# Attention pair on one core: the short turn of the products moved by one, and head weighing tied to VectorE's copies

## The chip, the core and the metric

The kernel runs on one core of a Trainium2 chip. TensorE (PE) multiplies into PSUM; its weight loads are listed as PEld. ScalarE (ACT) does most exponentials. VectorE (DVE) copies, and does a few exponentials by arithmetic. GpSimd (POOL) masks and weighs heads. SyncE (SP) issues the transfers. The metric is device time in microseconds (us) of one launch; the kernel before takes 1421.66 us, the median of three runs (1420.84 to 1422.12).

## The reference

Two attention layers over 2048 tokens of width 576 with 32 heads of 18, side by side in the output:

```python
def _A_ref(x, wq, wk, wv, wo):           # one key and value head for all 32 query heads
    scores = jnp.einsum("bhqd,bkd->bhqk", q, k) * (Dh ** -0.5)
    p = _softmax(scores, axis=-1)
    o = jnp.einsum("bhqk,bkd->bhqd", p, v)
    return o.transpose(0, 2, 1, 3).reshape(B, S, H * Dh) @ wo
...
def _B_ref(x, wq, wk, wv, wo, beta):     # causal within 4 segments of 512, and a memory of the segments before
    for s in range(N):
        p = _softmax(logits, axis=-1)
        a_dot = jnp.einsum("bhqk,bhkd->bhqd", p, vs)
        a_mem = num / den
        o = g * a_mem + (1.0 - g) * a_dot
        ...
    return o @ wo
...
return jnp.concatenate([a, b], axis=-1)
```

## The kernel before

The first part of the program (up to about 290 us) projects queries, keys and values, and sums the memory of B. The second part is the attention. It is cut into **blocks**: 32 A blocks (512 queries of 4 heads against all 2048 keys) and 32 B blocks (512 queries of 4 heads within their segment). B blocks come in pairs, put behind 13 of the A blocks by the list `after`.

A block is made of **items**. An item of scores is a key tile of 128 and a pair of heads: two matmuls into a score buffer E (three buffers in PSUM), then an exponential into a tile P. An A block has 32 such items, a B block 6. An item of products is a key tile and a half of the queries: four matmuls, one for each head, of P with the values, added up in O. There are as many items of products as of scores.

The work goes in **turns**, written out by the main loop (the order on TensorE, ScalarE and VectorE is the order in the code). A turn k does the scores of `turns[k]`, then their exponentials, then a piece of the output projection (`run_fill`, the filler F), then one step of VectorE's own exponential if one stands in the list `slow`, then the products of `prods[k - 2]`. `split` cuts a block's items into threes; where two are left over, as in A, that short turn is put at the place `cut`. For A, `turns` has it at place 10, the last of eleven turns, and `prods` at place 8. I number a block's turns from 0.

Of a turn's three score items, the first and the third go from E through ScalarE straight into P. The second is first copied by VectorE into a tile W, which frees E early, and ScalarE reads W last. In turn 0 of an A block the second item is VectorE's: it computes the exponential in one instruction on E (tile PD) and six later steps (`exponentials`), which the loop takes one at a turn.

When a chunk of 512 queries has all its heads, the **planner** (`at`, `due`, `finish`) loads the sums and the heads, and asks GpSimd to weigh each of five tiles of heads (`weigh`: one product for A and for the first segment of B, two products and a sum for the others). `due` takes at most two weighing steps in a turn (`heavy = 2`), and none when one of the next three turns has B blocks. GpSimd's instructions are kept in program order, but start as soon as what they wait for is there. The weighed heads are what the filler multiplies with the output weights. GpSimd also masks the exponentials of B on the diagonal (L941).

Lines of the profile: L918 and L927 scores of A and B, L936 ScalarE's exponentials, L933 the copy W, L894 to L901 VectorE's exponential, L966 products, L975 the copy of O, L773 filler, L797 its copy, L761 weighing.

Of the kernel before, what the change touches and what calls it, by code (L numbers as in the profile page):

```python
# [74 lines left out]
def attention_pair_kernel(ctx, tc, a_xT, a_w, a_wo, b_xT, b_w, b_wo, b_beta, ident_d, hmask_d, bmask_d, cmask_d, sel_d, zmask_d, selx_d, sely_d, out):  # L75
    nc = tc.nc
# [79 lines left out]
    with ExitStack() as ph:  # L156
# [248 lines left out]
        for s in range(NSEG):  # L405
# [110 lines left out]
            if not last:  # L516
                e = p2.tile([128, 4, DH], F32, name="ph31")
# [92 lines left out]
    with tc.If(loose > 0, preferred_fallthrough_block=False):  # L610
        with ExitStack() as ph:
# [37 lines left out]
            with tc.For_i(0, H, 1) as h:  # L649
# [5 lines left out]
                for i in range(NKT):  # L655
                    s, j = divmod(i, 4)
                    n = 128 * (j + 1)
# [97 lines left out]
    def weigh(ab, c, t, tiles):  # L755

        o, (rb, *mem) = parts[ab, c][: RT[t], t], [x[: RT[t]] for x in tiles]

        def step(dst, a, b, op):

            return lambda: tc.keep_in_program_order(nc.gpsimd.tensor_tensor(dst, a, b, op=op))  # L761

        steps = [step(o, o, rb, ALU.mult)]
        if mem:
            nb, rb2 = mem
            steps += [step(nb, nb, rb2, ALU.mult), step(o, o, nb, ALU.add)]
        return steps
# [117 lines left out]
        vseg[s] = v  # L885


    slow, now = [], [0]

    def exponentials(p, e):  # L890

        y, u, w = p.bitcast(U32), pp.tile([128, 2, 512], F32, name="n", bufs=1), pp.tile([128, 2, 512], F32, name="q", bufs=1)
        v, stt = nc.vector, nc.vector.scalar_tensor_tensor
        v.tensor_scalar(y, e, EXP_A, EXP_B, op0=ALU.mult, op1=ALU.add)  # L894
        steps = [
            lambda: v.tensor_scalar(u.bitcast(U32), y, MANTISSA, ONE_BITS, op0=ALU.bitwise_and, op1=ALU.bitwise_or),
            lambda: v.tensor_scalar(w.bitcast(U32), y, EXPONENT, None, op0=ALU.bitwise_and),
            lambda: stt(p, u, POLY[0], u, op0=ALU.add, op1=ALU.mult),
            lambda: stt(p, p, POLY[1], u, op0=ALU.add, op1=ALU.mult),
            lambda: stt(p, p, POLY[2], p, op0=ALU.add, op1=ALU.mult),  # L900
            lambda: stt(p, p, POLY[3], w, op0=ALU.add, op1=ALU.mult),  # L901
        ]
        slow.extend((now[0] + 2 + i, p, step) for i, step in enumerate(steps))

    def scores(it, pr, copied):

        ab, c, hg, kt = it
        st = stacks[ab, c, hg // 2]
        h = 2 * (hg % 2) + pr
        e = psE.tile([128, 2, 512], F32, name="E")  # L910
        dve = ab == "A" and (kt, pr) in BY_DVE
        p = pp.tile([128, 2, 512], F32, name="PD" if dve else "P", bufs=1 if dve else PBUFS)
        state[it, pr] = p
        n = 512 if ab == "A" else 512 - 128 * kt if kt < 2 else 384
        if ab == "A":
            for j, r0 in enumerate(HALF):
                rows = slice(r0, r0 + KR)
                nc.tensor.matmul(e[:, j], kstA[rows, 128 * kt : 128 * kt + 128], st[rows, h, :], start=True, stop=True)  # L918
            if (kt, pr) in BY_DVE:
                exponentials(p, e)  # L920
                return lambda: None
        else:
            for k, c0 in BKEYS[kt]:
                ks = slice(128 * k, 128 * k + 128)
                for j, r0 in enumerate(HALF):
                    rows = slice(r0, r0 + KR)
                    nc.tensor.matmul(  # L927
                        e[:, j, c0 : c0 + 512 - 128 * k], st[rows, 4 + h, ks], st[rows, h, 128 * k :], start=True, stop=True
                    )
        src = e  # L930
        if copied:
            src = pp.tile([128, 2, 512], F32, name="W", bufs=2)
            nc.vector.tensor_copy(src[:, :, :n], e[:, :, :n])  # L933

        def exponential():
            nc.scalar.activation(p[:, :, :n], src[:, :, :n], AF.Exp, scale=SCALE)  # L936
            if ab == "B":

                m = len(BKEYS[kt])
                diag = p.rearrange("p a (b t) -> p a b t", t=256)[:, :, 0:m, 0:128]  # L940
                nc.gpsimd.affine_select(  # L941
                    diag, diag, pattern=[[0, 2], [0, m], [1, 128]], base=0, channel_multiplier=-1, compare_op=ALU.is_ge, fill=0.0
                )

        return exponential
# [61 lines left out]
    turns, prods = [], []  # L1007
# [5 lines left out]
    def due(k, most=2, heavy=2):  # L1013

        cost = 0

        near = [its[n][0] for t in turns[k : k + 3] for n, pr in t]
        heavy *= "B" not in near
        for e in [e for e in later if e[0] <= k]:
            if most and cost + e[1] <= heavy and e[2]():  # L1020
                later.remove(e)
                e[3](k)
                cost += e[1]
                most -= 1
        return cost
# [53 lines left out]
    def split(n, cut):  # L1079

        sizes = [3] * (n // 3)
        if n % 3:
            sizes.insert(cut, n % 3)
        return [sum(sizes[:i]) for i in range(len(sizes) + 1)]

    with tc.manual_schedule(engines={ENG.PE, ENG.Activation, ENG.DVE}):
# [3 lines left out]
        for n, b in enumerate(blocks):  # L1090
            ms = [m for m in range(len(its)) if block_of[m] == n]
            items = [(m, k) for m in ms for k in range(2)]
            for out_, cut in ((turns, len(items) // 3), (prods, len(items) // 3 - 2)):
                at_ = split(len(items), cut)
                out_ += [items[a:z] for a, z in zip(at_, at_[1:])]
        at(ASK + 4, 0, lambda: True, lambda k: load_qf(2))
# [13 lines left out]
        for k in range(len(turns) + 2):  # L1110
            now[0] = k
            exps = [scores(its[n], pr, i == 1) for i, (n, pr) in enumerate(turns[k])] if k < len(turns) else []
            for i in (0, 2, 1) if len(exps) == 3 else range(len(exps)):
                exps[i]()
            if memory is None:
                run_fill()
            elif k >= ASK and all(its[n][0] == "A" for n, pr in turns[k]) and next(memory, None) is None:
                memory = None

            ends = k > 1 and any(hf and its[n][3] == (NKT - 1 if its[n][0] == "A" else 2) for n, hf in prods[k - 2])  # L1120
            if slow and (slow[0][0] <= k or not ends):
                slow.pop(0)[2]()
            for n, hf in prods[k - 2] if k > 1 else []:
                ab, c = its[n][:2]
                hg = products(its[n][:3], its[n][3], hf)
                if hg in (6, 7):
                    finish(k, ab, c, hg)
                if hg == 7 and ab == "B" and c + 1 < NSEG:
                    load_vseg(c + 1)
            due(k)  # L1130
            if k == len(turns):
                halve_w(0)
            for n, pr in turns[k] if k < len(turns) else []:
                it = its[n]
                ab = it[0]
                if pr == 0:
                    prefetch(ab, keys[ab].index((ab, it[1], it[2] // 2)) + 2)
                    if it in (("A", 0, 2, 8), ("A", 0, 5, 8)):
                        load_wo(*(("B", b_wo) if it[2] == 2 else ("A", a_wo)))

        while fill and fill[0][0] in begun:
            due(k, 4)
            run_fill()
            if filled[0] % FILL == 0:
                fill.pop(0)
            k += 1
# [25 lines left out]
        for t in range(5):  # L1172
            if t:
                halve_w(t)
            due(k, 4)
            k += 1
            halve_heads(rows[0], t)
# [5 lines left out]
        for n, key in enumerate(rows):  # L1183
            end = key == rows[-1]
            banks = [psE.tile([128, 2, 512], F32, name="E") for _ in range(3)]
            dst = [bk[:, hf, :288] for bk in banks for hf in range(2)]
# [75 lines left out]
```

## Time and profile before

| | us |
|---|---|
| median of three runs | 1421.66 |
| the profiled execution, time | 1422.47 |
| the profiled execution, span | 1420.7 |
| TensorE busy | 1404.0 |
| ScalarE busy | 1205.4 |
| VectorE busy | 964.4 |
| GpSimd busy | 244.6 |

The granted clock of TensorE was 0.997 of full speed over the span. A row of a timeline gives the start, the time that it took, engine, line, operation, tiles, shapes and count, and in brackets the engine's idle time before it with what ended it. On ScalarE and TensorE an instruction overlaps the next one, so the distance of two starts is the cost of one. A matmul of the products has two records in the trace, so an item of products (four matmuls) stands there as eight. In a row of groups or of a line's view the numbers behind a name are idle time in us and how often.

### The profile page before, as it was taken

Reading aid. Unit: us, or ns where it says so; the run is one execution under the profiler, and the core shown is the slowest. Engines: PE = TensorE matmul, PEld = TensorE weight load, DVE = VectorE, ACT = ScalarE, POOL = GpSimd, SP = SyncE. Lnnn points to the kernel's source line nnn. Section 1 sums busy time; section 2 is a strip of 40 time slices with the busy share of each in tenths; the row PEclk is TensorE's granted clock in tenths of the full one; section 3 lists DMA queues with packets and bytes.
Section 4 is the critical chain, followed back from the end, with each engine's and each line's share of the span. In section 5 each row is a group of like instructions: output and inputs, shape, how many; then the busy total and the mean of one; then the engine's idle time right before and its main releaser. Section 6 shows DMA issues by size and latency. Waiting matters only on the chain.

```text
span 1420.7 us, 39951 instructions
## 1 busy us (share of the span) xinstructions
PE 1404.0 (99%) x17132; PEld 843.3 (59%) x17132; DVE 964.4 (68%) x1157; ACT 1205.4 (85%) x1447; POOL 244.6 (17%) x326
## 2 busy tenths in 40 slices
PE   9999999999999999999999999999999999999998
PEld 6788888745555555555555555555555555555558
DVE  6656456456677767776766777666767766777663
ACT  4543434479999999999999999999999999999991
POOL 2431000003313213221110160131011400100002
PEclk9999999999999999999999999999999999999999
DMA  9766546557564535332312543232104221110013
GB/s 283 253 216 188 166 146 214 174 171 214 156 214 159 165 120 166 91 109 77 110 58 70 166 128 92 62 107 80 51 34 132 67 76 44 60 45 18 9 59 112
DMA packets 90720, 172.63 MB, mean 122 GB/s; under 512 B 14576, under 2 KB 22889, under 8 KB 90110
## 3 DMA queue, kind: packets, MB, share of 16 engines
q1 hardware_dynamic: 84122, 160.01, 36.0%
q0 software_dynamic: 1664, 4.78, 1.3%
q10 hardware_dynamic: 4752, 5.24, 1.1%
q8 instruction: 135, 2.21, 0.7%
q14 instruction: 47, 0.39, 0.1%
HBM read 99.32 MB, written 70.67 MB: 120 GB/s over the span
## 4 chain that ended last, share of the span: by engine, by line
PE 68%; ACT 7%; issue 2%; DMA 1%; DVE 1%; SPq 0%; ACTq 0%; DVEq 0%
PE O L966 31%; PE E L918 20%; PE F L773 11%; ACT P L936 7%; PE E L927 3%; PE E L1163 2%; PE F L829 1%; DMA stB<-qB 0%; DVE W L933 0%; PE F L1163 0%; PE O L1163 0%; DMA oA<-oe 0%; DMA stB<-kB 0%; DMA sm<-oA 0%; SPq L696 0%
## 5 line engine op out<-in xcount | busy, mean ns | idle before, releaser
L936 ACT ACTIVATE P<-E 128x1024 f32<-128x1024 f32 (+1 forms) x800 | 780.8, 1059 | 12.7 <-PE E L918 12.3
L933 DVE COPY W<-E 128x1024 f32<-128x1024 f32 (+1 forms) x384 | 461.2, 1201 | 248.8 <-PE E L918 189.2
L966 PE MATMUL O<-P,VA 128*32 128x256 f32 x7936 | 508.8, 380 | 0.0
L936 ACT ACTIVATE P<-W 128x1024 f32<-128x1024 f32 (+1 forms) x384 | 426.3, 1110 | 3.4 <-DVE W L933 3.2
L966 PEld LDWEIGHTS O<-P,VA 128*32 128x32 f32 x7936 | 262.2, 110 | 147.6 <-issue 6.6
L918 PE MATMUL E<-stA,kstA 56*128 56x512 f32 x1920 | 329.4, 439 | 1.8 <-DVE W L933 1.1
L918 PEld LDWEIGHTS E<-stA,kstA 56*128 56x128 f32 x1920 | 154.7, 184 | 178.2 <-ACT P L936 113.7
L941 POOL TENSOR_SCALAR_AFFINE_SELECT P<-P 128x256 f32<-128x256 f32 (+1 forms) x192 | 95.0, 495 | 480.3 <-ACT P L936 446.9
L761 POOL TENSOR_TENSOR o<-o,rb 126x512 f32<-126x512 f32 (+1 forms) x55 | 79.9, 1468 | 408.9 <-DMA o<-oA 146.0
L773 PE MATMUL F<-woB,o 126*32 126x192 f32 (+1 forms) x1920 | 127.4, 338 | 0.3 <-DVE osb L797 0.3
L966 PE MATMUL O<-P,vseg 128*32 128x256 f32 (+2 forms) x1536 | 81.8, 344 | 0.8 <-issue 0.8
L773 PEld LDWEIGHTS F<-woB,o 126*32 126x32 f32 (+1 forms) x1920 | 38.2, 108 | 70.6 <-issue 63.6
L975 DVE COPY oe<-O 128x512 f32<-128x512 f32 x64 | 44.3, 692 | 41.8 <-PE O L966 41.0
L252 PE MATMUL pj<-xh,wBl 128*126 128x512 f32 x180 | 72.4, 403 | 0.0
L252 PE MATMUL pj<-xh,wBh 128*126 128x512 f32 x180 | 71.9, 400 | 0.0
L121 ACT CAST qp<-pj 126x512 fp32r<-126x512 f32 (+1 forms) x54 | 31.0, 585 | 46.1 <-DVE kmB L450 32.4
L966 PEld LDWEIGHTS O<-P,vseg 128*32 128x32 f32 x1536 | 49.1, 109 | 25.4 <-issue 2.9
L773 PE MATMUL F<-woA,o 126*32 126x192 f32 (+1 forms) x960 | 63.9, 338 | 0.0
L927 PE MATMUL E<-stB 56*128 56x256 f32 (+3 forms) x512 | 61.3, 347 | 1.4 <-ACT P L936 0.9
L122 DVE TENSOR_TENSOR qp<-pj,qp 126x512 fp32r<-126x512 f32 (+1 forms) x54 | 36.7, 685 | 35.6 <-ACT qp L121 35.3
L252 PE MATMUL pj<-xl,wBh 128*126 128x512 f32 x144 | 57.3, 399 | 0.0
L927 PEld LDWEIGHTS E<-stB 56*128 56x128 f32 x512 | 38.6, 185 | 31.1 <-ACT P L936 20.8
(194 smaller groups left out, 1387.8 us busy)
## 6 DMA issues: line engine op xcount, KB each, us to landing
stB<-kB SPq DMA_DIRECT2D x96, 144.0 KB
stB<-qB SPq DMA_DIRECT2D x32, 288.0 KB
stA<-qA SPq DMA_DIRECT2D x30, 288.0 KB
oA<-oe SPq DMA_DIRECT2D x32, 256.0 KB
oB<-oe SPq DMA_DIRECT2D x32, 256.0 KB
qA<-qp SPq DMA_DIRECT2D x16, 504.0 KB
kB<-qp SPq DMA_DIRECT2D x16, 504.0 KB
qB<-qp SPq DMA_DIRECT2D x16, 504.0 KB
```

What stands on the lines that cost most here:

```text
L121: hold(nc.scalar.copy(qp[:R, 0, :n], src))
L122: hold(nc.vector.tensor_tensor(qp[:R, 1, :n], src, qp[:R, 0, :n].bitcast(F32), op=ALU.subtract))
L252: nc.tensor.matmul(dst, w[:, c0 : c0 + M], x, start=i == 0, stop=i == len(ops) - 1)
L761: return lambda: tc.keep_in_program_order(nc.gpsimd.tensor_tensor(dst, a, b, op=op))
L773: nc.tensor.matmul(dst[32 * j : 32 * j + 32], parts[ab, c][: RT[t], t, r0 : r0 + 32], wo[ab][: RT[t], t, c0 : c0 + n], start=start, stop=stop,
L918: nc.tensor.matmul(e[:, j], kstA[rows, 128 * kt : 128 * kt + 128], st[rows, h, :], start=True, stop=True)
L927: nc.tensor.matmul(e[:, j, c0 : c0 + 512 - 128 * k], st[rows, 4 + h, ks], st[rows, h, 128 * k :], start=True, stop=True)
L933: nc.vector.tensor_copy(src[:, :, :n], e[:, :, :n])
L936: nc.scalar.activation(p[:, :, :n], src[:, :, :n], AF.Exp, scale=SCALE)
L941: nc.gpsimd.affine_select(diag, diag, pattern=[[0, 2], [0, m], [1, 128]], base=0, channel_multiplier=-1, compare_op=ALU.is_ge, fill=0.0)
L966: nc.tensor.matmul(o[32 * j : 32 * j + 32, q0 : q0 + n], v, p[:, j % 2, p0 : p0 + n], start=m == hf == 0, stop=last and hf == 1,)
L975: nc.vector.tensor_copy(osb, o)
```

## The change

Three edits. The cut for the products' short turn moves from place 8 to place 9 of eleven; with the lag of two turns its products are multiplied in the first turn of the following block, where they were in the last turn of their own. A weighing step on GpSimd waits for the newest copy W that the loop has issued (`gate`). And `due` takes no weighing step when an entry of `slow` is due in this turn or the next.

```diff
         def step(dst, a, b, op):
 
-            return lambda: tc.keep_in_program_order(nc.gpsimd.tensor_tensor(dst, a, b, op=op))
+            def run():
+                ins = tc.keep_in_program_order(nc.gpsimd.tensor_tensor(dst, a, b, op=op))
+                if gate:
+                    tc.add_manual_dep(ins.ins, gate[-1].ins.name, AFTER, reason="beside the copies of this turn")
+
+            return run
...
-    slow, now = [], [0]
+    slow, now, gate = [], [0], []
+    AFTER = mybir.DependencyInfo(mybir.DependencyClass.Sync, mybir.DependencyReason.SCHED_ONLY)
...
-            nc.vector.tensor_copy(src[:, :, :n], e[:, :, :n])
+            gate.append(nc.vector.tensor_copy(src[:, :, :n], e[:, :, :n]))
...
-        heavy *= "B" not in near
+        heavy *= "B" not in near and all(e[0] > k + 1 for e in slow)
...
-            for out_, cut in ((turns, len(items) // 3), (prods, len(items) // 3 - 2)):
+            for out_, cut in ((turns, len(items) // 3), (prods, len(items) // 3 - 1)):
```

What that does to the order. First TensorE from an A block to the next (turn 10 of (A,3,2) and turn 0 of (A,3,3)). E with stA are scores, F the filler, O the products; PD is the tile that VectorE filled. Before:

```order
L918 MATMUL E<-stA,kstA 128x512 x4
L773 MATMUL F<-woB,o 32x192 x4
L966 MATMUL O<-P,VA 32x256 x2
L966 MATMUL O<-PD,VA 32x256 x2
L966 MATMUL O<-P,VA 32x256 x2
L966 MATMUL O<-PD,VA 32x256 x2
L918 MATMUL E<-stA,kstA 128x512 x6
L773 MATMUL F<-woB,o 32x192 x4
L966 MATMUL O<-P,VA 32x256 x12
```

and now:

```order
L924 MATMUL E<-stA,kstA 128x512 x4
L778 MATMUL F<-woB,o 32x192 x4
L972 MATMUL O<-P,VA 32x256 x2
L972 MATMUL O<-PD,VA 32x256 x2
L972 MATMUL O<-P,VA 32x256 x2
L972 MATMUL O<-PD,VA 32x256 x2
L972 MATMUL O<-P,VA 32x256 x4
L924 MATMUL E<-stA,kstA 128x512 x6
L778 MATMUL F<-woB,o 32x192 x4
L972 MATMUL O<-P,VA 32x256 x8
```

One product item, four matmuls, has moved from behind the six score matmuls of turn 0 to ahead of them. Next TensorE from an A block to a B block ((A,2,4) to (B,3,6)), where E with stB are the scores of B, before:

```order
L966 MATMUL O<-PD,VA 32x256 x2
L927 MATMUL E<-stB 128x512 x4
L927 MATMUL E<-stB 128x384 x2
L773 MATMUL F<-woB,o 32x192 x4
L966 MATMUL O<-P,VA 32x256 x12
```

and now:

```order
L972 MATMUL O<-PD,VA 32x256 x2
L972 MATMUL O<-P,VA 32x256 x4
L933 MATMUL E<-stB 128x512 x4
L933 MATMUL E<-stB 128x384 x2
L778 MATMUL F<-woB,o 32x192 x4
L972 MATMUL O<-P,VA 32x256 x8
```

The same item stands ahead of the first scores of B. Last GpSimd at the weighing of the second segment of B, with the semaphores that each instruction waits for in brackets (DMAHW are transfers, Pool is GpSimd itself). Before:

```order
L761 TENSOR_TENSOR o<-o,rb 126x512 [waits DMAHW3_49,DMAHW4_49,DMAHW1_49,DVE_49]
L761 TENSOR_TENSOR rb<-rb 126x512 [waits DMAHW5_49,DMAHW2_49]
L761 TENSOR_TENSOR o<-o,rb 126x512 [waits DMAHW6_49]
L761 TENSOR_TENSOR o<-o,rb 126x512 [waits DMAHW1_49]
L761 TENSOR_TENSOR o<-o,rb 126x512 [waits Pool_49]
```

and now:

```order
L762 TENSOR_TENSOR o<-o,rb 126x512 [waits DMAHW3_49,DMAHW4_49,DMAHW1_49,DVE_49]
L762 TENSOR_TENSOR rb<-rb 126x512 [waits DMAHW5_49,DMAHW2_49,DVE_49]
L762 TENSOR_TENSOR o<-o,rb 126x512 [waits DMAHW6_49]
L762 TENSOR_TENSOR o<-o,rb 126x512 [waits DMAHW1_49,DVE_49]
L762 TENSOR_TENSOR o<-o,rb 126x512 [waits Pool_49]
```

The instructions and their order are the same; the first of each turn now also waits for VectorE (a second one in the same turn stands behind it).

## The prediction

> **What bounds the kernel now.** I read the page first, then the busy time of a late stretch, then the timeline of TensorE, ScalarE and VectorE over one joint between two A blocks, then the same joint from A to B, then a stretch in which GpSimd weighs heads.
>
> The page's first part:
>
> ```profile
> PE 1404.0 (99%) x17132; PEld 843.3 (59%) x17132; DVE 964.4 (68%) x1157; ACT 1205.4 (85%) x1447; POOL 244.6 (17%) x326
> ```
>
> and one row of the busy-time view by stretches (its columns are PE, PEld, DVE, ACT, POOL, then granted clock and DMA):
>
> ```profile
> 1150.00:1250.00 100.00, 100.00 (x1418) 52.41 (x1410) 73.47 (x74) 99.28 (x108) 7.12 (x5) 1.00 0.18 53
> ```
>
> In the attention part TensorE and ScalarE are both filled. So neither bounds alone; they wait for each other at certain turns. The timeline of TensorE shows where. These are turns 9 and 10 of block (A,3,2), then turns 0, 1 and the start of turn 2 of (A,3,3). A turn begins with its scores (E, L918), then one piece of the output projection (F, L773), then its products (O, L966):
>
> ```profile
> 1227.34 1.08 PE L918 MATMUL E<-stA,kstA 56*128 56x512 f32 x6
> 1230.11 0.72 PE L918 MATMUL E<-stA,kstA 56*128 56x512 f32 x4
> 1230.76 0.53 PE L773 MATMUL F<-woA,o 72*32 72x192 f32 x8
> 1232.09 1.21 PE L918 MATMUL E<-stA,kstA 56*128 56x512 f32 x6
> 1233.23 0.53 PE L773 MATMUL F<-woB,o 126*32 126x192 f32 x8
> 1233.58 1.48 PE L966 MATMUL O<-P,VA 128*32 128x256 f32 x24
> 1234.99 0.96 PE L918 MATMUL E<-stA,kstA 56*128 56x512 f32 x6
> 1237.64 0.96 PE L918 MATMUL E<-stA,kstA 56*128 56x512 f32 x6
> ```
>
> Starts of E give the turns: turn 9 2.77 us, turn 10 1.98, turn 0 2.90, turn 1 2.65. Three scores cost 0.96 us when nothing holds them (turn 1), and 1.21 in turn 0: there TensorE waits about 0.25 us for a score buffer. ScalarE at the same place:
>
> ```profile
> 1230.39 1.21 ACT L936 ACTIVATE P<-W 128x1024 f32<-128x1024 f32 x1
> 1231.34 1.17 ACT L936 ACTIVATE P<-E 128x1024 f32<-128x1024 f32 x1
> 1232.24 1.21 ACT L936 ACTIVATE P<-W 128x1024 f32<-128x1024 f32 x1
> 1233.19 2.10 ACT L936 ACTIVATE P<-E 128x1024 f32<-128x1024 f32 x2
> 1235.53 1.94 ACT L936 ACTIVATE P<-E 128x1024 f32<-128x1024 f32 x2 [0.25 <-PE E L918]
> ```
>
> ScalarE's exponentials overlap: they follow each other by 0.90 us after one that reads E and by 0.95 after one that reads W (1231.34 to 1232.24, 1230.39 to 1231.34). Turns 1 to 9 hold three of them, 2.75 us. Turns 0 and 10 hold two, since VectorE does one of turn 0. Left alone, the exponential of 1235.53 would have followed at about 1233.19 + 0.90 + 0.92 = 1235.01. So ScalarE runs dry for about half a microsecond at every such joint; the page's "idle" of 0.25 is only what stands beyond the overlap. The path through a joint is: ScalarE's exponential at 1231.34 frees a score buffer, TensorE finishes the scores of turn 0, the filler, three products, the first score of turn 1, and then ScalarE starts, 0.54 us after that turn began (1234.99 to 1235.53). From there to turn 10 ScalarE is never dry and holds TensorE (2.77 instead of 2.65).
>
> **The products' short turn.** An A block has 32 score items and 32 product items, in ten turns of three and one of two. The scores' short turn is the block's last. Products lag two turns, and their list had its short turn at place 8, so it fell on turn 10, beside the short scores. Now it stands at place 9 and falls on the next block's first turn. One product item moves from turn 0 into turn 10. Nothing is added; the stores and the copy of the finished O stay in turn 1.
>
> What an item costs: turn 1 (three scores, three products, 2.65 us) less turn 10 (two and two, 1.98) is 0.67 us. The score's share is 0.96 - 0.72 = 0.24, so a product item is 0.43 us.
>
> Between two A blocks. Turn 10 becomes 1.98 + 0.43 = 2.41 us, and turn 0's scores start at 1232.52 in place of 1232.09. The buffer that held them is free when the exponential of 1231.34 is done, at 1231.34 + 1.17 = 1232.51; the second score needs it at 1232.52 + 0.24 = 1232.76, so the wait of 0.25 goes. Turn 0 then takes 2.65 - 0.43 = 2.22 us and turn 1 starts at 1234.74, not at 1234.99: **0.25 us gained**. What is late next? ScalarE's first exponential of turn 0 can start at 1232.52 + 0.54 = 1233.06, ahead of 1233.19 where ScalarE comes free, so it isn't starved there. In turn 1 ScalarE starts 0.54 after 1234.74, still some 0.27 later than it could: the joint stays TensorE's and the whole 0.25 shows. There are 18 joints from A to A (32 A blocks, 13 of them followed by B, and the last): 18 x 0.25 = 4.5 us. The two product items left in turn 0 need exponentials of turn 9, the last at 1230.39, long done.
>
> From A to B. The scores of an A block's turn 10, of the first and the second B turn behind it, and of the second B block's first turn:
>
> ```profile
> 1045.92 0.73 PE L918 MATMUL E<-stA,kstA 56*128 56x512 f32 x4
> 1047.91 1.13 PE L927 MATMUL E<-stB 56*128 56x512 f32 x6
> 1050.73 0.85 PE L927 MATMUL E<-stB 56*128 56x384 f32 x10
> 1053.27 0.90 PE L927 MATMUL E<-stB 56*128 56x512 f32 x6
> ```
>
> and ScalarE in turn 1 of the next A block:
>
> ```profile
> 1061.08 1.02 ACT L936 ACTIVATE P<-E 128x1024 f32<-128x1024 f32 x1 [0.56 <-PE E L918]
> ```
>
> The same six matmuls take 1.13 us after A and 0.90 later: 0.23 us is a wait that a product item in front of it would fill. Behind it TensorE sets the pace until ScalarE runs dry at the next A block's turn 1 (0.56 idle), so 0.23 us stays gained. The first three joints from A to B lie where the chain that ended last runs on ScalarE (two of its rows):
>
> ```profile
> 370.25 2.26 ACT P L936 x3
> 418.71 2.26 ACT P L936 x3
> ```
>
> There I count nothing. Ten are left: 10 x 0.23 = 2.3 us. From B to A nothing changes: B's six items have no short turn. Sum of this part: **-6.8 us**.
>
> **The planner's new term** (`heavy` off while an exponential step is due within a turn). Stepping through the rules: a step is due at block turn + 2 + i, but is taken as soon as a turn doesn't end a block's products; step 0 goes in turn 0, step i in turn i + 1. When `due` asks in any turn the next step's number is always at least k + 2, so the term never says no. The weighing steps stand in the same turns as before, 29 of the 65 ahead of the last rows in turns 2 to 6, which hold exponential steps. This edit costs and brings nothing, and the change doesn't do this half of what it says.
>
> **The added wait.** What the wait does change is when GpSimd starts. Before, a weighing step ran as soon as its data had landed; now it also waits for the copy W of its turn. Behind it on GpSimd stand further weighing steps and, at the next B block, the masks (L941); the planner keeps three turns free ahead of B, so the masks don't queue behind it. GpSimd in turns 3 to 5 of (A,1,6):
>
> ```profile
> 825.66 3.52 POOL L761 TENSOR_TENSOR rb<-rb 126x512 f32<-126x512 f32 x2
> 829.15 4.58 POOL L761 TENSOR_TENSOR o<-o,rb 126x512 f32<-126x512 f32 x2
> ```
>
> VectorE beside it:
>
> ```profile
> 825.89 2.16 DVE L898 SCALAR_TENSOR_TENSOR PD<-n 128x1024 f32<-128x1024 f32 x1
> 827.97 1.21 DVE L933 COPY W<-E 128x1024 f32<-128x1024 f32 x1
> 829.10 1.21 DVE L899 SCALAR_TENSOR_TENSOR PD<-PD,n 128x1024 f32<-128x1024 f32 x1
> 830.24 1.21 DVE L933 COPY W<-E 128x1024 f32<-128x1024 f32 x1
> 831.37 1.21 DVE L900 SCALAR_TENSOR_TENSOR PD<-PD 128x1024 f32<-128x1024 f32 x1
> ```
>
> and ScalarE, with the exponential that came late:
>
> ```profile
> 826.95 1.97 ACT L936 ACTIVATE P<-E 128x1024 f32<-128x1024 f32 x2
> 829.21 1.06 ACT L936 ACTIVATE P<-W 128x1024 f32<-128x1024 f32 x1 [0.29 <-DVE W L933]
> ```
>
> A step that VectorE starts while GpSimd is inside one (825.89, GpSimd since 825.66) takes 2.16 us; one that starts 0.05 us ahead of GpSimd's (829.10 against 829.15) takes 1.21, and then GpSimd's takes 2.3 (half of 4.58). The copy W takes 1.21 either way. So the later of the two waits. With the new wait GpSimd can start only after the copy's end, 830.24 + 1.21 = 831.45, and VectorE starts its next step at 831.37, ahead of it. GpSimd then loses, and nobody waits for GpSimd within two turns. The Trainium skill, SBUF — State Buffer, Who interferes with whom, says that a VectorE instruction with two SBUF inputs and a GpSimd one that reads SBUF exclude each other, and that issue order decides who blocks. By that rule a copy from PSUM is safe company for GpSimd and the exponential's steps aren't, and this wait takes GpSimd out of the copies and sets it beside the steps: the rule speaks against the edit if GpSimd should win the race. The rows agree with the rule.
>
> What the wait can bring is bounded by what ScalarE and TensorE now lose to a late W:
>
> ```profile
>   ACT P L936: 3.2, 8
>   PEld E L918: 3.0, 6
> ```
>
> (from the view of line L933, those who waited for it: us, times). Some of these are late for VectorE's own reasons. What it can cost: VectorE's step is 0.95 longer (2.16 - 1.21), and the exponential at 829.21 came 2.26 us after 826.95 where 1.81 was due: 0.45 lost, times 29 steps = 13 us. I take nothing for this part: GpSimd is behind in the race, and the gain is small. The ends, -3.2 and +13, stay for the range and the rivals.
>
> **Rivals.** (1) *The wait moves instead of going.* If turn 0's scores are still held, by a copy W or an exponential that now ends 0.25 us later than turn 0 reaches it, the product item is only moved. Against it: the buffer is free at 1232.51 and wanted at 1232.76. For it: the margin is just 0.25 us, and osb copies and late copies stand on VectorE. Half the joints lost gives -3.4, all lost 0: 1418.3 to 1421.7.
> (2) *Slower: GpSimd gets there first.* If GpSimd starts ahead of VectorE's step in the turns with steps, each of the 29 costs ScalarE 0.45 us: +13 - 6.8 = +6.2, 1427.9 us. It decides when GpSimd's start is less than 0.08 us after the copy's end in place of behind the step (831.37 against 831.45). For it: two weighing steps stand in many turns, and the second can run into the next turn's step. Against it: after a loss GpSimd ends in the next turn's copy, which it doesn't hurt.
> (3) *The joint closes fully.* If ScalarE weren't starved at all, 18 x 0.5 + 10 x 0.56 = 14.6 us would go: 1407.1. Against it: TensorE's own work up to turn 1 stays.
>
> **How the numbers follow.** The profiled execution took 1422.47 us with a span of 1420.7; the median of three runs is 1421.66, so the sum is taken off the median: 1421.66 - 6.8 = **1414.9 us**. Chances: this forecast 0.68, rival 1 0.16, rival 2 0.12, rival 3 0.04. The range goes down by the wait's bound, 1414.9 - 3.2 = 1411.7, and up into rival 1, to 1420.5; rivals 2 and 3 and the rest of rival 1 are left out. A run of this kernel can tell about 0.2%, 2.8 us, so 1418.8 parts faster from same: faster is 0.68 + 0.04 + a third of rival 1, 0.77; same is the rest of it, 0.11; slower 0.12.
>
> **What would show it.** Right: at the joints turn 10 lasts about 2.4 us and turn 0 about 2.2, turn 0's scores take 0.96, ScalarE's idle at turn 1 falls from 0.25 to about 0; the first B scores after A take 0.90. GpSimd's steps begin after the copies, at 1.3 or 2.3 us each, and VectorE's steps stay at 1.21. Wrong: scores of turn 0 that still take 1.2, steps L898 to L901 above 2 us more often than now, or more time in which ScalarE waits for W.

## The result, and the profile after

| | before | after |
|---|---|---|
| median of seven runs | 1422.12 us (1419.49 to 1423.55) | 1417.49 us (1416.72 to 1419.29) |
| ratio, 95% interval | | 0.9979 [0.9969, 0.9988] |
| profiled execution: time, span | 1422.47, 1420.7 | 1417.8, 1416.1 |

The change makes the kernel faster by about 3.0 us (0.0021 x 1421), 1.7 to 4.4 by the interval. That ratio is the estimate on record and not the quotient of the two medians, which would be 0.9967, 4.63 us; I go by the record, and the same cut alone (e1 below, over more runs) gives 3.08 us by its medians. The forecast was 6.8 us: right in direction, less than half delivered. The busy times of TensorE, ScalarE and GpSimd hardly moved, and VectorE's fell by 8.0 us. The first part of the page after, then the same late stretch of the view by stretches:

```profile
PE 1401.8 (99%) x17132; PEld 844.6 (60%) x17132; DVE 956.4 (68%) x1157; ACT 1206.1 (85%) x1447; POOL 247.5 (17%) x326
1150.00:1250.00 100.00, 100.00 (x1430) 52.80 (x1422) 73.68 (x74) 99.98 (x109) 0.00 (x0) 1.00 0.16 50
```

ScalarE's share of that stretch rose from 99.28 to 99.98: the dry moments that the busy time shows are gone. The joint from (A,3,2) to (A,3,3) on TensorE, turns 9, 10, 0, 1 and 2 (scores are L924 now):

```profile
1225.04 1.08 PE L924 MATMUL E<-stA,kstA 56*128 56x512 f32 x6
1227.81 0.72 PE L924 MATMUL E<-stA,kstA 56*128 56x512 f32 x4
1230.23 0.96 PE L924 MATMUL E<-stA,kstA 56*128 56x512 f32 x6
1232.45 1.08 PE L924 MATMUL E<-stA,kstA 56*128 56x512 f32 x6
1235.22 0.97 PE L924 MATMUL E<-stA,kstA 56*128 56x512 f32 x6
```

Turn 10 lasts 2.42 us, turn 0 2.22, and turn 0's scores take 0.96 as if nothing held them: the forecast, within a hundredth. But turn 1 now lasts 2.77, where it was 2.65, since its scores take 1.08 in place of 0.96. Half of what turn 0 no longer waits for, turn 1 waits for: its third score needs the buffer that ScalarE reads in turn 0's last exponential. That exponential, and the weight load of the third score, which waits for ScalarE:

```profile
1231.81 1.17 ACT L942 ACTIVATE P<-E 128x1024 f32<-128x1024 f32 x1
1233.03 0.19 PEld L924 LDWEIGHTS E<-stA,kstA 56*128 56x128 f32 x2 [0.29 <-ACT P L942]
```

The exponential ends at 1232.98 and the load starts 0.05 us later. ScalarE (L936 in before, L942 in after), in before and then in after: the exponential of turn 1 that reads W, and the one behind it, the first of turn 2.

```profile
1237.36 1.06 ACT L936 ACTIVATE P<-W 128x1024 f32<-128x1024 f32 x1
1238.30 1.95 ACT L936 ACTIVATE P<-E 128x1024 f32<-128x1024 f32 x2
```

```profile
1234.81 1.06 ACT L942 ACTIVATE P<-W 128x1024 f32<-128x1024 f32 x1
1235.82 1.02 ACT L942 ACTIVATE P<-E 128x1024 f32<-128x1024 f32 x1
```

In before, turn 2's first exponential followed the one that reads W after 0.94 us, its normal pitch; in after, after 1.01 (1234.81 to 1235.82), because turn 2's first score came late: at all 15 joints of this kind in the stretch below, that exponential starts 0.10 us behind the end of the score. So the joint brings 2.55 us at the W of turn 1 (1237.36 - 1234.81) over 2.30 at turn 9 (1227.34 - 1225.04), 0.25 as forecast, and one exponential later only 0.18 (2.48 over 2.30).

The joint from A to B, (A,2,4) to (B,3,6), on TensorE (the scores of B are L933): A's turn 10, the two turns of the first B block, and the second B block's first.

```profile
1044.21 0.73 PE L924 MATMUL E<-stA,kstA 56*128 56x512 f32 x4
1046.64 0.90 PE L933 MATMUL E<-stB 56*128 56x512 f32 x6
1048.79 1.11 PE L933 MATMUL E<-stB 56*128 56x384 f32 x10
1051.59 0.91 PE L933 MATMUL E<-stB 56*128 56x512 f32 x6
```

The first B scores take 0.90, as forecast, in place of 1.13. But the second B turn's take 1.11, where they took 0.85. From A's turn 10 to the second B block is 7.38 us (1051.59 - 1044.21); in before it was 7.35 (1053.27 - 1045.92). Nothing is kept. ScalarE's rows over the same joint say why. In before, first the exponential of A's turn 9 that reads W, then the last three of the two B turns, of which the third reads W too, and the first of the second B block:

```profile
1046.19 1.21 ACT L936 ACTIVATE P<-W 128x1024 f32<-128x1024 f32 x1
...
1051.53 1.69 ACT L936 ACTIVATE P<-E 128x768 f32<-128x768 f32 x2
1052.91 1.04 ACT L936 ACTIVATE P<-W 128x768 f32<-128x768 f32 x1
1053.81 1.75 ACT L936 ACTIVATE P<-E 128x1024 f32<-128x1024 f32 x2
```

and after:

```profile
1044.50 1.19 ACT L942 ACTIVATE P<-W 128x1024 f32<-128x1024 f32 x1
...
1051.22 1.02 ACT L942 ACTIVATE P<-W 128x768 f32<-128x768 f32 x1
1052.13 1.73 ACT L942 ACTIVATE P<-E 128x1024 f32<-128x1024 f32 x2
```

7.62 us in the one, 7.63 in the other. ScalarE ran at its own pace through the whole joint in before already, and was dry only at the end of it, ahead of the second B block (0.90 us from 1052.91 to 1053.81, and 0.91 in after, where 0.73 is enough when the scores come in time, as e4 below shows). TensorE's wait in the first B turn was a wait for an engine that was itself busy: taking it away lets TensorE arrive earlier and wait in the next turn.

To compare kernels over many joints I use one stretch, from the first score of turn 1 of (A,1,0) to that of turn 1 of (A,3,7). It holds 15 joints from A to A and 8 from A to B, and leaves out the first part of the program and the tail. Its end points on TensorE's timeline, before and after:

```profile
604.60 1.19 PE L918 MATMUL E<-stA,kstA 56*128 56x512 f32 x6
1351.00 0.95 PE L918 MATMUL E<-stA,kstA 56*128 56x512 f32 x6
```

```profile
604.00 0.73 PE L924 MATMUL E<-stA,kstA 56*128 56x512 f32 x4
1347.71 1.09 PE L924 MATMUL E<-stA,kstA 56*128 56x512 f32 x6
```

746.40 us before, 743.71 after: 2.69 gained. Cut at turn 1 of every A block, 3.06 of that lies in the 15 pieces from A to A and -0.37 in the 8 pieces that hold B blocks. Of the 15, 13 gain between 0.18 and 0.26; one gains 0.58, and one loses 0.20. Of the -0.37, -0.24 is the first piece: turn 1 of (A,1,0) lasts 3.11 us instead of 2.88 and gives back there what its joint had gained just ahead of the stretch. What lies outside the stretch differs between profiles by more than the change can explain: from the last point to the end of the span it is 69.7 us in before, 68.4 in after, and 68.3 to 70.1 over the experiments that leave the tail's work as it was.

### The profile page after: what moved, and what is told of

Read it like the earlier page. It is cut to its first block, busy times and chain, and to the rows that moved or that the text cites. A ratio compares the mean times of both kernels' runs of the same rounds, so it can differ in the third digit from the quotient of the medians.

```text
span 1416.1 us, 39968 instructions
## 1 busy us (share of the span) xinstructions
PE 1401.8 (99%) x17132; PEld 844.6 (60%) x17132; DVE 956.4 (68%) x1157; ACT 1206.1 (85%) x1447; POOL 247.5 (17%) x326
## 3 DMA queue, kind: packets, MB, share of 16 engines
q8 instruction: 135, 2.21, 0.7%
## 4 chain that ended last, share of the span: by engine, by line
PE 66%; ACT 10%; issue 3%; DVE 1%; POOL 0%; DVEq 0%; ACTq 0%
PE O L972 30%; PE E L924 19%; PE F L778 11%; ACT P L942 10%; PE E L933 3%; PE E L1169 2%; DVE W L939 1%; PE F L1169 0%; PE O L1169 0%; PE F L834 0%; DVE PD L900 0%; DVE PD L907 0%; DVE PD L905 0%; POOL P L947 0%; DVE osb L802 0%
## 5 line engine op out<-in xcount | busy, mean ns | idle before, releaser
L942 ACT ACTIVATE P<-E 128x1024 f32<-128x1024 f32 (+1 forms) x800 | 778.8, 1055 | 7.9 <-PE E L924 7.5
L942 ACT ACTIVATE P<-W 128x1024 f32<-128x1024 f32 (+1 forms) x384 | 424.8, 1106 | 2.3 <-DVE W L939 1.9
L924 PE MATMUL E<-stA,kstA 56*128 56x512 f32 x1920 | 325.6, 438 | 0.7 <-ACT P L942 0.2
L924 PEld LDWEIGHTS E<-stA,kstA 56*128 56x128 f32 x1920 | 154.7, 184 | 174.5 <-ACT P L942 128.1
L762 POOL TENSOR_TENSOR o<-o,rb 126x512 f32<-126x512 f32 (+1 forms) x55 | 83.4, 1529 | 442.4 <-DVE W L939 312.6
L933 PE MATMUL E<-stB 56*128 56x256 f32 (+3 forms) x512 | 61.9, 347 | 1.3 <-ACT P L942 0.6
L933 PEld LDWEIGHTS E<-stB 56*128 56x128 f32 x512 | 38.6, 185 | 31.6 <-ACT P L942 28.9
```

Source lines behind the costliest of these rows:

```text
L762: ins = tc.keep_in_program_order(nc.gpsimd.tensor_tensor(dst, a, b, op=op))
L933: nc.tensor.matmul(e[:, j, c0 : c0 + 512 - 128 * k], st[rows, 4 + h, ks], st[rows, h, 128 * k :], start=True, stop=True)
```

## Experiments

The ratio is to the kernel before, run beside each; "stretch" is the gain in the stretch above, by one profile each, as A to A plus A to B.

| kernel | median us | ratio, 95% interval | stretch gain us |
|---|---|---|---|
| after | 1417.49 | 0.9979 [0.9969, 0.9988] | 3.06 - 0.37 = 2.69 |
| e1_cut_alone | 1416.88 | 0.9981 [0.9972, 0.9989] | 3.45 - 0.36 = 3.09 |
| e2_gate_alone | 1420.41 | 1.0001 [0.9993, 1.001] | 0.27 + 0.15 = 0.42 |
| e3_cut_before_b | 1420.69 | 1.0005 [0.9997, 1.0014] | 0.61 + 0.02 = 0.63 |
| e4_mixed | 1415.52 | 0.9965 [0.9953, 0.9977] | 3.18 + 1.63 = 4.81 |
| e5_one_too_late | 1424.00 | 1.0022 [1.0013, 1.0031] | -2.46 + 0.22 = -2.24 |
| e6_free_turns | 1429.28 | 1.0059 [1.0042, 1.0075] | 3.18 - 0.02 = 3.15 |
| e7_light_apart | 1418.80 | 0.9985 [0.9976, 0.9994] | 2.11 + 1.05 = 3.17 |
| e8_light_apart_free | 1432.51 | 1.0068 [1.0048, 1.0088] | 2.64 + 1.58 = 4.22 |
| e9_mixed_free | 1415.07 | 0.9967 [0.9955, 0.9978] | 3.44 + 1.65 = 5.09 |
| e10_mixed_free_gate | 1415.23 | 0.9961 [0.9948, 0.9973] | 3.23 + 1.48 = 4.71 |

e2 and e3 change nothing between two A blocks, and still show 0.27 and 0.61 there. Most of it is one piece: from (A,1,6) to (A,1,7) both are 0.41 shorter than before, whose profile has the late copy there that the prediction shows (the exponential at 829.21). The 0.58 of after is that 0.41 and a joint like the others. A single stretch says nothing below about half a microsecond.

**The cut without the rest.** Against before:

```diff
-            for out_, cut in ((turns, len(items) // 3), (prods, len(items) // 3 - 2)):
+            for out_, cut in ((turns, len(items) // 3), (prods, len(items) // 3 - 1)):
```

> The cut of the products moved, without the wait on GpSimd. Theory A (a joint from A to A is worth 0.19 us, a joint from A to B nothing, because the wait for a score buffer only moves into the second B turn): 18 x 0.19 = 3.4 us less than before, ratio 0.9976; scores of the second B turn behind A take about 1.1 us where they took 0.86. Rival B (both joints are worth what was predicted, and the added wait on GpSimd ate the rest): 6.8 us less, ratio 0.9952. Rival C (the wait on GpSimd made the gain): no change, 1.000.

Measured 0.9981, the whole of the change. Every turn of the joints has the same lengths as in after.

**The rest without the cut.** Against after:

```diff
-            for out_, cut in ((turns, len(items) // 3), (prods, len(items) // 3 - 1)):
+            for out_, cut in ((turns, len(items) // 3), (prods, len(items) // 3 - 2)):
-        heavy *= "B" not in near and all(e[0] > k + 1 for e in slow)
+        heavy *= "B" not in near
```

> The wait on GpSimd alone, products cut as before. Theory A: 0 to 1 us less than before (late copies in some blocks gone, new ones in others), ratio 0.9993 to 1.0000. Rival B: 2 to 4 us more, ratio 1.0015 to 1.003. Rival C: 3 us less, 0.998.

Measured 1.0001: GpSimd's added wait alone moves nothing that can be told. By pieces it loses 0.33 from (A,2,7) to (A,3,0), where after loses its 0.20 and e1, without the wait, gains 0.18: the late copy there comes with the wait.

**The cut moved only ahead of B blocks.** `joint` is the kind of the next block; against before:

```diff
+            joint = blocks[n + 1][0] if n + 1 < len(blocks) else "A"
+            late = 2 if joint == "A" else 1
-            for out_, cut in ((turns, len(items) // 3), (prods, len(items) // 3 - 2)):
+            for out_, cut in ((turns, len(items) // 3), (prods, len(items) // 3 - late)):
```

> The cut moved only in A blocks that a B block follows, no wait on GpSimd. Theory A: 0, within 0.5 us, ratio 1.000; the first B scores fall to 0.90 us and the second B turn's rise to about 1.1. Rival B: 10 x 0.23 = 2.3 us less, ratio 0.9984.

Measured 1.0005 [0.9997, 1.0014], and 0.02 us over the 8 joints in the stretch: what the first B turn gains, the second gives back, each time. The term of 2.3 us is not there.

**Mixed: place 9 ahead of A, place 10 ahead of B.** If ScalarE is dry only behind the second B turn, the item must be taken out of that turn, not out of the first one. Against e3:

```diff
-            late = 2 if joint == "A" else 1
+            late = 1 if joint == "A" else 0
```

> Between A blocks the cut as in the change (short turn in the next block's first turn); ahead of a B block one place later still, so that the short turn of the products falls on the second B turn. No wait on GpSimd. Theory A: the second B turn is where TensorE is held and then starves ScalarE, so taking 0.43 us of products out of that turn pays 0.18 to 0.23 us at ten joints: 3.4 + 2.0 = 5.4 us less than before, ratio 0.9962. If the B joint is bound by ScalarE throughout: 3.4 less, 0.9976. If a late product there starves ScalarE in the first B turn: less than 3.4.

Measured 0.9965. The same joint in the timeline of TensorE (L918 and L927 again), and the two exponentials of ScalarE at its end:

```profile
1041.78 0.72 PE L918 MATMUL E<-stA,kstA 56*128 56x512 f32 x4
1044.20 0.90 PE L927 MATMUL E<-stB 56*128 56x512 f32 x6
1046.79 0.84 PE L927 MATMUL E<-stB 56*128 56x384 f32 x10
1048.89 0.90 PE L927 MATMUL E<-stB 56*128 56x512 f32 x6
```

```profile
1048.78 1.02 ACT L936 ACTIVATE P<-W 128x768 f32<-128x768 f32 x1
1049.51 1.90 ACT L936 ACTIVATE P<-E 128x1024 f32<-128x1024 f32 x2
```

From A's turn 10 to the second B block 7.11 us (1048.89 - 1041.78), 0.24 less than before; no scores are held, and ScalarE's last step is 0.73 us instead of 0.90. This version is faster than before beyond the noise. Its interval overlaps those of after and e1, so that it beats them too rests on the stretch: 1.63 us in the joints to B, 0.20 to 0.27 in each of seven of the eight pieces, where they have none.

**One place too late between A blocks.** Against e3:

```diff
-            late = 2 if joint == "A" else 1
+            late = 0 if joint == "A" else 2
```

> Ahead of an A block the short turn of the products one place later than in the change (it falls on the next block's turn 1), ahead of a B block as before; no wait on GpSimd. If the joint's path runs through TensorE from turn 10 to the first score of turn 1: turn 10 2.42 us, turn 0 2.65 us, together 5.07 where they were 4.88, so ScalarE starves 0.19 us longer and 18 joints cost 3.4 us: ratio 1.0024. If the short turn only had to leave turn 10 (any later place does): 3 us less, 0.998.

Measured 1.0022, slower. Turns 10, 0 and 1 of the same joint, and ScalarE in it:

```profile
1231.49 0.73 PE L918 MATMUL E<-stA,kstA 56*128 56x512 f32 x4
1233.91 0.95 PE L918 MATMUL E<-stA,kstA 56*128 56x512 f32 x6
1236.56 0.96 PE L918 MATMUL E<-stA,kstA 56*128 56x512 f32 x6
```

```profile
1237.10 1.94 ACT L936 ACTIVATE P<-E 128x1024 f32<-128x1024 f32 x2 [0.45 <-PE E L918]
```

The item is now taken from turn 1, behind the score on which ScalarE waits. Turns 10 and 0 are 5.07 us together (1236.56 - 1231.49), where they were 4.88 before (1234.99 - 1230.11) and are 4.64 in after (1232.45 - 1227.81). No score is held here, TensorE waits for nothing, and the kernel is slower: ScalarE is dry for 0.45 us by the bracket, 0.25 before. What pays is what stands ahead of the score that the dry engine waits for.

**A planner term that says no.** The change's `all(e[0] > k + 1 for e in slow)` never does. Here weighing is refused in a turn in which VectorE took a step (`now[1]`) or while one is pending; against after:

```diff
-    slow, now, gate = [], [0], []
+    slow, now, gate = [], [0, -1], []
...
-        heavy *= "B" not in near and all(e[0] > k + 1 for e in slow)
+        heavy *= "B" not in near and not slow and now[1] < k
...
                 slow.pop(0)[2]()
+                now[1] = k
```

> The changed kernel with a working form of the planner's term: no weighing step in a turn in which a step of VectorE's exponential is left or has just been done, so weighing falls on a block's turns 7 to 10; the wait on GpSimd stays. If the wait costs through weighing steps that get ahead of VectorE's step (about 0.6 to 0.8 us in the changed kernel beside the cut alone): 0.6 us less than the changed kernel, ratio 0.9976, and no step of L898 to L901 above 1.3 us ahead of the last rows. If the later weighing starves the filler: turns without filler, up to 2 us more.

A miss: 1.0059. The second case of the expectation, a starved filler, is the one that came, at 8 us in place of up to 2. No step of VectorE is stretched any more (0 of the 160 instructions of its exponential that take about 1.2 us alone stand above 1.35 us; 7 in before, 4 in after. Of the 64 that take 0.69 us alone, 8 took more than 1.0 in before, 1 in after, 0 here). But the last of the first five weighings is put off behind four B blocks, into (A,0,4), and 21 more turns than before have no filler. It is made up at the end. TensorE behind the last products, in after and in e6:

```profile
1375.82 1.48 PE L972 MATMUL O<-P,VA 128*32 128x256 f32 x24
1377.12 1.16 PE L778 MATMUL F<-woB,o 126*32 126x192 f32 x24
```

```profile
1372.72 1.48 PE L972 MATMUL O<-P,VA 128*32 128x256 f32 x24
1374.02 1.49 PE L778 MATMUL F<-woB,o 126*32 126x192 f32 x32
...
1386.43 3.43 PE L778 MATMUL F<-woB,o 126*32 126x192 f32 x40 [0.48 <-DVE osb L802]
```

24 filler records stand behind the last product in after, 192 here; it lasts to 1389.86 instead of 1378.28, although the products end 3.1 us earlier. The distance from the stretch's end to the span's end is 84.5 us instead of 68.4.

Not all of these 16 us are filler work. The view by stretches, e6 at that place:

```profile
1374.00:1390.00 16.00, 12.72 (x197) 7.21 (x189) 2.30 (x7) 3.61 (x7) 0.00 (x0) 0.71 0.13 47
```

TensorE's granted clock is 0.71 there and 0.78 from 1390 to 1400, where it is 1.00 in after; 40 filler records take 1.83 us at 1375.98 and 3.43 at 1386.43. The six runs of e6 part the same way: three of 1426.4 to 1427.6 us with a mean clock of 0.997, and three of 1430.9 to 1432.1, the profiled one among them, with 0.993 or 0.994. So by these runs about 5 us are the clock's, and the lower three still lie about 9 us above after (1426.56 against 1417.49). What lowered the clock is not shown.

**Free turns only where the filler isn't starved, without and with GpSimd's wait.** The term of e6 from turn 121 on, on top of the mixed cuts; e10 adds the change's wait.

```diff
-        heavy *= "B" not in near
+        heavy *= "B" not in near and (k < 121 or not slow and now[1] < k)
```

> The cuts of the mixed version (place 9 ahead of an A block, place 10 ahead of a B block), and from turn 121 on no weighing in a turn in which VectorE takes an exponential step or has one pending; GpSimd waits for nothing new. Theory A (few weighings ever meet a step at all: in the trace of the mixed version 7 of 160 steps are stretched, 4 of them after turn 121, and late copies W hold ScalarE up by 3.1 us there, 1.3 of it for other reasons by the trace of the version with free turns): 0 to 2 us below the mixed version, ratio to before 0.995 to 0.9965, and no step above 1.3 us after turn 121. Rival B (each of the weighings in step turns costs 0.45 us, as in the prediction's upper end): about 20 x 0.45 = 9 us below, ratio 0.990. Rival C (weighing later starves the filler): ratio 0.998 or more, with more than 24 filler matmul records behind the last product.

> The same with GpSimd's added wait for the newest copy W. Theory A (with free turns there is no step to race for, so the wait only delays weighing by up to a turn, and nobody waits for that): the same ratio as without the wait, within 0.0007. Rival B (the wait keeps costing where a filler's copy stands between W and the rest of the turn): 0.5 to 1 us slower than without it. Rival C (it still helps, by keeping GpSimd beside copies): 0.5 to 1 us faster.

0.9967 and 0.9961, with 24 filler records at the end again; neither can be told from the mixed version, nor from each other. One expectation failed: without the wait 3 of the long steps behind turn 121 are still stretched. The weighings stand in free turns in the program, but GpSimd runs ahead of it: those of the second B segment start in turns 1 to 10 of (A,1,6), as their heads land. With the wait they start in turns 7 to 10 of that block and 0 and 7 to 10 of the next, and no step behind turn 121 is stretched. So only the term and the wait together keep weighing out of the steps' turns, and that is worth less than these runs can tell: a stretched step is rare.

**The short turns apart.** The scores' short turn at place 7 instead of 10 (the mixed cuts for the products; `LATE`, the place of VectorE's tile in the products' order, goes from 12 to 8), so that TensorE's and ScalarE's light turns don't stand side by side. e8 adds the wait and the term of e6.

```diff
-            for out_, cut in ((turns, len(items) // 3), (prods, len(items) // 3 - late)):
+            for out_, cut in ((turns, len(items) // 3 - 3), (prods, len(items) // 3 - late)):
```

> The short turn of the scores at place 7 of an A block instead of the last, so that the two turns in which ScalarE has only two exponentials (7 and 0) no longer stand side by side; VectorE's tile is used at place 8 of the products instead of 12; products cut as in e4_mixed; no wait on GpSimd. If the loss at a joint is that three score buffers can't carry ScalarE over two light turns in a row: ScalarE no longer starves at turn 1 between A blocks (0.32 us left of it in the changed kernel), so 18 x (0.19 + 0.30) + 10 x 0.24 = 11 us less than before, ratio 0.992. If ScalarE starves at turn 7 instead: as e4_mixed, 0.9965. If TensorE has to wait for exponentials of the same turn, its products being a place too early: slower than before, above 1.00.

> e7_light_apart together with the wait on GpSimd and the working form of the planner's term (e6_free_turns). If weighing in turns without exponential steps keeps GpSimd and VectorE apart: up to 1 us less than e7_light_apart, ratio 0.9915; if it makes no difference, the same as e7_light_apart.

Both missed: 0.9985 and 1.0068. e8 carries the tail of e6 (84.5 us, with the same fall of the clock: 0.75 from 1374 to 1390). In e7 turns 0, 1 and 2 of (A,3,3) on TensorE, and on ScalarE the W of turn 1 with the exponential behind it:

```profile
1230.18 0.96 PE L918 MATMUL E<-stA,kstA 56*128 56x512 f32 x6
1232.39 1.26 PE L918 MATMUL E<-stA,kstA 56*128 56x512 f32 x6
1235.35 0.96 PE L918 MATMUL E<-stA,kstA 56*128 56x512 f32 x6
```

```profile
1234.76 1.12 ACT L936 ACTIVATE P<-W 128x1024 f32<-128x1024 f32 x1
1235.89 1.94 ACT L936 ACTIVATE P<-E 128x1024 f32<-128x1024 f32 x2
```

Turn 0 keeps its 2.21 us and ScalarE isn't dry ahead of turn 1, but the third score of turn 1 now waits 0.30 us for its buffer (1.26 against 0.96), and the first exponential of turn 2 comes 1.13 us after the W before it, 0.18 late. The wait of the joint has moved into turn 1 once more, whole. What the earlier place of VectorE's tile costs wasn't separated from that, so the rest of e7's shortfall stays open.

## Why the prediction missed

*What bounds the kernel, and the item.* Right: 0.43 us for an item gives turn 10 as 2.41 and turn 0 as 2.22, and the rows say 2.42 and 2.22.

*Between two A blocks, 18 x 0.25.* The mechanism held and the size was off. The gain is 0.25 as far as ScalarE's start in turn 1, and 0.18 one exponential later. Over the stretch it is 3.06 in after and 3.45 in e1. Without the 0.41 of before's own late copy, and without the 0.38 that after loses beside e1 to a late copy from (A,2,7) to (A,3,0), both are 3.03 to 3.04: 0.20 for each of 15. With the joint into (A,1,0), which keeps nothing, left out, 17 joints bring about 3.4 us, not 4.5. The sentence that was wrong is "the whole 0.25 shows": I asked what was late next in turn 0 and at the first score of turn 1, and not at its third. That score needs the buffer of turn 0's last exponential. ScalarE isn't dry in turn 0, so this exponential starts no earlier for the change, and TensorE, which comes 0.25 earlier, meets it (1232.98 against 1233.03 in the rows of after).

*From A to B, "so 0.23 us stays gained", 10 x 0.23.* This step failed. e3 does it alone and brings nothing, and ScalarE's 7.62 and 7.63 us show that TensorE didn't set the pace there. Rival 1 had the right mechanism for this half, but with the wrong place: not a copy W or an exponential that ends late in turn 0, but the next turn's scores. The rows that would have shown it lay in the profile of before, one engine further than I read: from ScalarE's W of turn 9 at 1046.19 to the W at 1052.91, behind which the gap stands, there are eight exponentials at their normal pitch (3 x 0.95 + 2 x 0.90 + 3 x 0.69 = 6.72 us = 1052.91 - 1046.19; the 0.69 of B's shorter ones is half of 1051.53 to 1052.91, and the same in after and e4), so a TensorE wait inside that time couldn't be on the path. e4, which takes the item out of the turn that stands ahead of the gap, keeps 1.63 over 8 joints, 0.20 each. With the two terms as measured, 3.4 + 0 = 3.4 against 3.0 of the ratio, inside its interval.

*The planner's term costs and brings nothing.* Right by the placement: the weighing steps stand in the same turns, and e6 shows what a term that says no would have done, to the tail above all.

*The added wait, 0 between -3.2 and +13.* The value held: e2 is 1.0001, and e10 against e9 shows no difference. The reason was only half right. GpSimd does not always lose the race. VectorE and GpSimd in turns 3 to 5 of (A,2,7), after:

```profile
1123.08 1.23 DVE L939 COPY W<-E 128x1024 f32<-128x1024 f32 x1 [0.83 <-ACT P L942]
1124.22 0.35 DVE L802 COPY osb<-F 128x192 f32<-128x192 f32 x1
1124.49 2.27 DVE L904 SCALAR_TENSOR_TENSOR PD<-n 128x1024 f32<-128x1024 f32 x1
1126.68 1.21 DVE L939 COPY W<-E 128x1024 f32<-128x1024 f32 x1
1127.82 1.21 DVE L905 SCALAR_TENSOR_TENSOR PD<-PD,n 128x1024 f32<-128x1024 f32 x1
```

```profile
1124.39 1.29 POOL L762 TENSOR_TENSOR o<-o,rb 126x512 f32<-126x512 f32 x1 [8.72 <-DVE W L939]
1127.97 2.20 POOL L762 TENSOR_TENSOR rb<-rb 126x512 f32<-126x512 f32 x1 [2.30 <-DVE W L939]
```

and ScalarE behind the late copy:

```profile
1127.93 1.06 ACT L942 ACTIVATE P<-W 128x1024 f32<-128x1024 f32 x1 [0.26 <-DVE W L939]
```

Both outcomes stand here one turn apart. The copy of 1123.08 ends at 1124.31, and GpSimd starts 0.08 later. In that turn a filler's copy (osb) stands between W and the step, the step comes at 1124.49, behind GpSimd, and takes 2.27 us; the next W is late and ScalarE idles. In the next turn nothing stands between, VectorE's step starts at 1127.82, ahead of GpSimd's 1127.97, and GpSimd takes the 2.20. That is rival 2's mechanism, but not at its stated point: GpSimd starts 0.08 us behind the copy's end in both turns, and what decides is whether a filler's copy puts VectorE's step off. It happens in few turns, 4 stretched steps in 160, against 7 in before and 5 to 8 in the experiments that have neither the wait nor the term of e6. Three of the four have osb's copy just ahead of them; at the fourth (861.52) GpSimd was inside the second of two weighing steps, as rival 2 also feared. The wait does shorten what is stretched: with the short steps counted, 15 instructions of VectorE's exponential took some 11.5 us too long in before (10 to 14 and 6.5 to 10.4 us in those experiments), and 5 took some 4.4 in after, the same in e2. In the time, e2 shows nothing of it. The Trainium skill, SBUF — State Buffer, Who interferes with whom, has issue order decide who blocks; both turns agree (1124.39 ahead of 1124.49, 1127.82 ahead of 1127.97). Of the ends, what a late W costs is read from the view of the copy's line, those who waited for it, in after:

```profile
  POOL o L762: 312.6, 19
...
  ACT P L942: 1.9, 6
  PEld E L924: 1.9, 6
```

ScalarE's 3.2 us became 1.9. GpSimd's 312.6 cost nobody anything that e2 can tell, as assumed.

## What to carry to other kernels

A wait is worth something only if the engine that it feeds runs dry behind it: follow the other engine's starts through the whole stretch first, and move work away from ahead of the score that the dry engine waits for, not out of the turn where the wait happens to be seen. When a wait goes, look for the next one as far as the run-ahead of the buffers reaches (here three scores, so into the next turn's third), since a freed buffer shifts all of them. A rule that holds work back from bad moments needs a look at who lives on that work; here the filler did, and the tail grew by 16 us in the profiled execution, some 5 of them by a lowered clock, to save a few stretched steps whose removal e9 and e10 couldn't show in the time.

## What was not expected of the hardware

In these rows two instructions of VectorE follow each other sooner than GpSimd can follow the first one. The copy of 1126.68 ends at 1127.89, VectorE's next step starts at 1127.82 and GpSimd, released by the same copy, at 1127.97. So GpSimd, waiting for VectorE's instruction, comes behind the next instruction of VectorE by 0.15 us, and an instruction as short as osb's (0.35 us by its row, 0.27 from start to start) in between turns the order round.
